# One decode step on one core: w_down's product on two partitions, one copy of it per engine, and the rounds of V in runs with the wait between them

## The chip, the cores and the metric

One NeuronCore of a Trainium2 chip. The metric is the device time of one execution in microseconds. The *span* of a trace runs from the first to the last instruction of the program that the trace records. All runs below are "fast" (none lies over 1.5% above the fastest of its kernel).

## The reference

One token goes through a pre-norm attention over a cache of 65,536 positions (8 key/value heads, 32 query heads, head size 128) and a gated block with its residual:

```python
q = (layernorm(x) @ wq)                      # x: [1, 1, 512], wq: [512, 4096]
scores = einsum("bhqd,bhkd->bhqk", q, k) * 128 ** -0.5
o = einsum("bhqk,bhkd->bhqd", softmax(scores), v)
h = x + o.reshape(1, 1, 4096) @ wo           # wo: [4096, 512]
z = layernorm(h)
out = h + (sigmoid(z @ w_gate) * (z @ w_up)) @ w_down   # F = 1792
```

K and V together are 268 MB in bf16, so this is above all a stream from memory.

## The kernel before

SyncE issues all large loads on one queue. For each head K comes in three loads and V in three (in four for the last head). VectorE transposes K by chunks, PE multiplies, ScalarE takes the exponential. The product with V runs in *rounds*: eight matmuls of 512 columns, four column groups at a time. A head has 16 rounds, ten in its first part and six in its fourth; between the sixth and the seventh, and between the fourteenth and the fifteenth, there may be a wait for the next load of V. In the code, `p` counts the rounds and is compared with `c` in every round to find the place of the wait:

```python
def waits():                       # stands away from the loop
    e.reg_alu(c, c, 8, ALU.add)
    ...                            # which wait it is; last head: "L" or "VL"
    nc.br("products", engines=here)

goto("sums", "values")             # a round begins
pv_regs(e)                         # 14 register operations: addresses
away("br_eq", p, c, "waits", waits, "products")
goto("products", "sums")
section("B")                       # eight matmuls of V
mm_at(e, ps(5, 0, 504, 96, 128), ..., kept=True)      # a spare matmul
e.reg_alu(p, p, s, ALU.add)        # ... four register operations
e.br_ne(m, 0, on_true="sums", on_false="sums_end")
```

A *spare matmul* computes nothing that is used; it is there to keep PE busy, and so its clock up. `warm(e, n)` issues n such ones of 504 columns.

The end of the kernel, after the last head (shortened):

```python
# gate and up: [1, 448] in each of four column groups, 32 matmuls
e.matmul(ps(bank, 0, FG, 32*c, 32*c + 1), lhsT=hc[:, kt:kt + 1], rhs=..., tile_position=(0, 32*c))
e.matmul(ps(YB, 0, 128), lhsT=gsel[:, :], rhs=hz[:, :], ...)      # the residual h
...                                                               # tanh, product: hh
e.transpose(hhT[:, :], hh[:, :])
# w_down: 14 row blocks r (three loads: 8, 4 and 2 blocks) x 4 column groups g
e.matmul(ps(YB, 0, 128, 32*g, 32*g + 1), lhsT=hhT[:, 32*r:32*r + 1], rhs=wd_v[:, r, g*128:(g + 1)*128], tile_position=(0, 32*g))
# g 0 and 1 copied by VectorE, 2 and 3 by ScalarE, then one row out
e.dma_start(out[0], y_sb[:, :])
```

Of the kernel before, what the change touches and what calls it, by code (L numbers as in the profile page):

```python
# [6 lines left out]
bf16 = mybir.dt.bfloat16  # L7
# [10 lines left out]
D = 512  # L18
# [197 lines left out]
def bass_sequential_preLN__gqa_block_cached__glu_gated_glu__decode_kernel(  # L216
# [21 lines left out]
    with ExitStack() as es:  # L238
# [42 lines left out]
        L_sb = sb("L_sb", [128, 4], fp32)  # L281
        lsum = sb("lsum", [128, 1], fp32)
        rl = sb("rl", [128, 1], fp32)
        hc = sb("hc", [128, 4], bf16)
        sg = sb("sg", [128, FG], fp32)
        sg2 = sb("sg2", [128, FG], fp32)
        hh = sb("hh", [128, FG], bf16)
        hhT = sb("hhT", [128, FG], bf16)
        y_sb = sb("y_sb", [1, D], bf16)

        W0 = NKT * CH
        Lw = [sb(f"Lw{i}", [128, n * DH // RW], bf16) for i, (_, n) in enumerate(WO)]
# [66 lines left out]
        op("pool", lambda e: e.iota(iota_i[:, :], [[1, 128]], base=128, channel_multiplier=-1), name="iota")  # L359
        for nm, t, v in (("onesf", onesf[:, :], 1.0), ("xz0", xz[:, :], 0.0), ("onef", one_f[:, :], 1.0), ("nhalf", nhalf[:, :], -0.5),  # L360
                         ("gs0", gsel[:, :], 0.0), ("zcol", zcol[:, :], 0.0), ("qh0", qh[:, :], 0.0), ("qz0", qz[:, :], 0.0),
                         ("PTz", PT_sb[:, 4 * 512:PT_ROW], 0.0), ("Wz", ktw[:, W0:KTW_ROW], 0.0)):
            op("pool", lambda e, t=t, v=v: e.memset(t, v), name=nm)
        op("dve", lambda e: e.tensor_scalar(ident[:, :], iota_i[:, :], 128.0, None, op0=ALU.is_equal), ["iota"], "ident")
        op("dve", lambda e: e.tensor_scalar(identf[:, :], iota_i[:, :], 128.0, None, op0=ALU.is_equal), (), "identf")
# [6 lines left out]
                                          bass.AP(tensor=head_of, offset=0, ap=[[4, 128], [0, 16], [1, 4], [0, 2]])), ["head"], "lsel")  # L372
        op("dve", lambda e: e.tensor_reduce(row_of[:, :], identf[:, :].rearrange("p (c r) -> p r c", r=RW), AX.X, ALU.max), (), "row")
        op("dve", lambda e: e.tensor_reduce(blk_of[:, :], identf[:, :].rearrange("p (c r) -> p c r", r=RW), AX.X, ALU.max), (), "blk")
        op("dve", lambda e: e.tensor_reduce(bass.AP(tensor=gsel, offset=0, ap=[[128, 128], [32, 4]]),
                                            identf[:, :].rearrange("p (s j) -> p s j", s=4), AX.X, ALU.add), ["gs0", "identf"], "gsel")



# [282 lines left out]
        def pe_flow(e, section):  # L662
            later = []

            def away(op, reg_, value, name, body, back=None):
                getattr(e, op)(reg_, value, on_true=name, on_false=f"{name}_not")
                later.append((name, body, back or f"{name}_not", blocks[-1][0]))
                label(f"{name}_not")

            i, w, p, v, m, c, s = (R.setdefault(n, e.alloc_register(f"r_{n}")) for n in "iwpvmcs")  # L670
            w0, p0 = addr_of(ktw, W0 + NC - 1 + 127), addr_of(PT_sb, 31 * 4)
            v_at = [addr_of(ring, j * CH) for j in AT["V"]]
            step = (2 * 2 * 512, 2 - 2 * 2 * 512)
            lag = v_at[0] - addr_of(ring, AT["V7"][0] * CH)
            i_last = v_at[0] - lag
            i_first = i_last + HKV * lag
            e.reg_mov(i, i_first)
            e.reg_mov(s, step[0])
            goto("head")
            e.reg_mov(w, w0)  # L680
            e.reg_mov(p, p0)
            e.reg_mov(c, p0 + 6)
            e.reg_alu(v, i, v_at[0], ALU.min)
            goto("part")
            e.br_eq(i, i_last, on_true="values", on_false="scores")
            label("scores")
            for half in range(NC // NR):
                for je in range(4):
                    if half or je:
                        e.reg_alu(reg(e, half * 4 + je), w, 2 * (je * WJ - half), ALU.add)  # L690
            away("br_eq", w, w0, "first_scores", lambda: section("As"), "more_scores")
            section("An")
            goto("more_scores", "scores")
            section("A")
            e.br_eq(i, i_first, on_true="next", on_false="values")
            label("values", "part")
            e.reg_mov(m, PARTS[0])
            warm(e, 3)
            away("br_eq", w, w0, "values0", lambda: section("V0"), "sums")
            e.br_ne(w, w0 - 12, on_true="next", on_false="values3")  # L700
            label("values3")
            e.reg_mov(v, v_at[2])
            e.reg_mov(m, PARTS[3])
            section("V3")
            goto("sums", "values")
            pv_regs(e)

            def last_second():
                section("L")

            def waits():
                e.reg_alu(c, c, 8, ALU.add)
                e.br_eq(w, w0, on_true="second", on_false="fourth")
                label("second", "waits")
                away("br_eq", i, i_last, "rows_of_o", last_second, "products")
                section("V2")
                nc.br("products", engines=here)
                label("fourth", "waits")
                e.br_ne(i, i_last, on_true="products", on_false="last_rounds")
                label("last_rounds", "fourth")  # L720
                section("VL")

            away("br_eq", p, c, "waits", waits, "products")
            goto("products", "sums")
            section("B")
            mm_at(e, ps(5, 0, 504, 96, 128), at_reg(PT_sb, reg(e, 11), [[PT_ROW, 128], [4, 32]]), e.lower_ap(qz[:, 0:504]), True, 32, 96, kept=True)
            e.reg_alu(p, p, s, ALU.add)
            e.reg_alu(s, s, step[0] ^ step[1], ALU.bitwise_xor)
            e.reg_alu(v, v, 2 * 2 * CH, ALU.add)
            e.reg_alu(m, m, -1, ALU.add)  # L730
            e.br_ne(m, 0, on_true="sums", on_false="sums_end")
            label("sums_end")
            def outs():
                warm(e, 2)
                section("O")
                warm(e, 1, load=False)

            away("br_eq", w, w0 - 12, "outs", outs)
            goto("next", "part")
            e.reg_alu(w, w, -4, ALU.add)  # L740
            e.br_ne(w, w0 - 16, on_true="part", on_false="head_end")
            label("head_end")
            e.br_eq(i, i_last, on_true="after", on_false="more_heads")
            label("more_heads")
            section("X")
            e.reg_alu(i, i, -lag, ALU.add)
            nc.br("head", engines=here)
            for name, body, back, under in later:
                label(name, under)
                body()  # L750
                nc.br(back, engines=here)
            label("after", "head_end")
# [11 lines left out]
        for i in range(HKV + 1):  # L764
            loop, last = 0 < i < HKV, i == HKV
            for r in range(NR):
# [27 lines left out]
                if not last and r == 3:  # L794
# [2 lines left out]
        P.part = {}  # L797
        regroup(1)
        project(range(NQ - GS, NQ), O3, ["O3.1", "wo1"], last=True)
        op("pe", lambda e: warm(e, 1, load=False))  # L800


        ln_stats(1, lambda e: e.tensor_tensor(hT[1][:, :], ps(YT, 0, 4), x_col[:, :], ALU.add), "yT", STB, 0)
        op("dve", lambda e: e.scalar_tensor_tensor(hc[:, :], ps(STB, 0, 1).to_broadcast([128, 4]), -1.0 / D, hT[1][:, :],
                                                   op0=ALU.mult, op1=ALU.add), ["tot.1"], "hc")
        op("dve", lambda e: e.tensor_tensor(hz[:, :].rearrange("p (j k) -> p j k", k=4),
                                            bass.AP(tensor=sel_f, offset=0, ap=[[32, 128], [1, 32], [0, 4]]),
                                            bass.AP(tensor=hT[1], offset=0, ap=[[4, 128], [0, 32], [1, 4]]), ALU.mult),
# [3 lines left out]
        for i, (nm, bank) in enumerate((("wg", GB), ("wu", UB))):  # L812
            at = W_AT[nm]
            for kt in range(4):
                for c in range(4):
                    dep = [f"{nm}.{j}" for j, (k0, _) in enumerate(W_SPLIT[nm]) if k0 == kt and c == 0]
                    op("pe", lambda e, at=at, kt=kt, c=c, bank=bank: e.matmul(  # L817
                        ps(bank, 0, FG, 32 * c, 32 * c + 1), lhsT=hc[:, kt:kt + 1],
                        rhs=ring[:, at + kt * FF + c * FG: at + kt * FF + (c + 1) * FG],
                        start=(kt == 0), stop=(kt == 3), tile_position=(0, 32 * c)),  # L820
                       ["hc"] * (kt == 0 and c == 0) + dep, f"gu{i}" if kt == 3 and c == 3 else None)
# [5 lines left out]
        op("dve", lambda e: e.tensor_tensor(hh[:, :].rearrange("p (r q) -> p r q", r=NF),  # L827
                                            ps(UB, 0, FG).rearrange("p (q r) -> p r q", r=NF),
                                            sg2[:, :].rearrange("p (q r) -> p r q", r=NF), ALU.mult), ["gu1", "sg2"], "hh")
        op("dve", lambda e: e.transpose(hhT[:, :], hh[:, :]), ["hh"], "hhT")  # L830
        for i, (r0, r1) in enumerate(WD_SPLIT):
            for r in range(r0, r1):
                for g in range(4):
                    last = r == NF - 1 and g == 3
                    op("pe", lambda e, r=r, g=g: e.matmul(  # L835
                        ps(YB, 0, 128, 32 * g, 32 * g + 1), lhsT=hhT[:, 32 * r:32 * r + 1], rhs=wd_v[:, r, g * 128:(g + 1) * 128],
                        start=False, stop=(r == NF - 1), tile_position=(0, 32 * g), skip_group_check=True),
                       ["hhT", f"wd{i}"] if r == r0 and g == 0 else (), "y" if last else None)
        for g in (0, 2, 1, 3):
            if g < 2:  # L840
                op("dve", lambda e, g=g: e.tensor_copy(y_sb[:, 128 * g:128 * g + 128], ps(YB, 0, 128, 32 * g, 32 * g + 1)), ["y"], f"ysb{g}")
            else:
                op("act", lambda e, g=g: e.activation(y_sb[:, 128 * g:128 * g + 128], ps(YB, 0, 128, 32 * g, 32 * g + 1), AF.Copy),
                   ["y"], f"ysb{g}")
        dma("sp", lambda e: e.dma_start(out[0], y_sb[:, :]), "out", [f"ysb{g}" for g in range(4)], "out")
        P.at_end = ("out",)
        P.emit()

# [27 lines left out]
```

## Time and profile before

| | |
|---|---|
| device time, median of 6 | 657.81 us (657.55 to 658.58) |
| span of the profiled run | 656.2 us |
| moved from memory | 282.33 MB, 430 GB/s over the span |
| end of the stream of loads | 653.5 us |
| mean granted PE clock | 0.872 |
| PE busy | 460.9 us (70%), of it 53.1 in the spares of the rounds |

The prediction shows the lines on which this rests: the DMA row, and the windows and the timeline of the end.

### The profile page before, as it was taken

The numbers are of one execution on the slowest core, as the hardware profiler recorded it, in microseconds if no ns is written. First come the engines' busy times: TensorE is split into PE (matmuls) and PEld (weight loads), VectorE is DVE, ScalarE is ACT, GpSimd is POOL, SyncE is SP. The second block draws the span as 40 slices with busy tenths as digits, with TensorE's granted clock in tenths as the row PEclk, the third lists the DMA queues.
The fourth block names the chain that finished last, engine by engine and source line by source line (L and its number), as shares of the span: only waits on it lengthen the run. The fifth ranks groups of instructions, "written<-read, shape, count | busy, mean of one in ns | idle before, by whom it ended". The sixth has DMA issues, their size and how long they took to land.

```text
span 656.2 us, 6578 instructions
## 1 busy us (share of the span) xinstructions
PE 460.9 (70%) x2564; PEld 73.8 (11%) x1587; DVE 350.2 (53%) x432; ACT 42.9 (7%) x114; POOL 3.6 (1%) x17
## 2 busy tenths in 40 slices
PE   0688587857669567786677676695767966777776
PEld 0200010011001010010100111010100101001122
DVE  1299846747266645647258380684536572573202
ACT  1100200020000200001000200002000020001001
POOL 1000000000000000000000000000000000000000
PEclk9989799788889697896887988787978978879798
DMA  9999999999999999999999999999999999999998
GB/s 400 431 447 431 425 421 431 431 437 433 455 431 431 431 415 434 440 443 433 421 447 431 431 423 447 446 434 437 399 447 431 431 431 431 460 434 411 425 429 348
DMA packets 8498, 282.33 MB, mean 430 GB/s; under 512 B 1073, under 2 KB 1074, under 8 KB 1586
## 3 DMA queue, kind: packets, MB, share of 16 engines
q1 hardware_dynamic: 8354, 282.33, 99.6%
q10 hardware_dynamic: 144, 0.00, 0.0%
HBM read 282.33 MB, written 0.00 MB: 430 GB/s over the span
## 4 chain that ended last, share of the span: by engine, by line
DMA 54%; PE 26%; DVE 12%; issue 6%; ACT 1%; PEldq 0%; PEld 0%; SPq 0%
DMA ring<-in_A_k_cache_dram 33%; PE PS L415 22%; DMA ring<-in_A_v_cache_dram 19%; DVE ktw L504 11%; DMA x_col<-in_A_x_dram 2%; PE PS L423 2%; ACT P_sb L550 1%; PE PS L817 0%; DVE PT_sb L560 0%; DVE M_sb L511 0%; PE PS L660 0%; PEldq L171 0%; PE PS L835 0%; PE PS L386 0%; PE PS L544 0%
## 5 line engine op out<-in xcount | busy, mean ns | idle before, releaser
L504 DVE STREAM_TRANSPOSE ktw<-ring 128x1024 f32<-128x1024 f32 x256 | 292.3, 1207 | 152.2 <-DMA ring<-in_A_k_cache_dram 152.2
L415 PE MATMUL PS<-ktw 128*128 128x512 bf16 x1024 | 287.1, 430 | 103.2 <-DVE ktw L504 86.0
L415 PE MATMUL PS<-ring,PT_sb 128*32 x1024 | 90.5, 423 | 52.6 <-PEq L171 26.8
L415 PEld LDWEIGHTS PS<-ktw 128*128 x256 | 26.7, 104 | 343.6 <-issue 246.4
L415 PE MATMUL PS<-qz,PT_sb 128*32 128x504 bf16 x128 | 53.1, 415 | 0.0
L415 PEld LDWEIGHTS PS<-ring,PT_sb 128*32 x1024 | 25.0, 115 | 134.7 <-issue 131.0
L593 ACT ACTIVATE po_sb<-PS,rl 128x512 bf16<-128x512 f32 x8 | 5.5, 687 | 524.1 <-PE PS L415 524.1
L423 PE MATMUL PS<-qz,ident 128*128 128x504 bf16 x121 | 33.7, 374 | 2.1 <-issue 2.1
L511 DVE TENSOR_REDUCE M_sb<-PS 128x1 f32<-128x512 f32 x32 | 19.9, 683 | 22.4 <-PE PS L415 22.4
L539 DVE TENSOR_REDUCE gmj<-PS 1x4 f32<-1x128 f32 x8 | 2.2, 279 | 46.0 <-PE PS L537 46.0
L550 ACT ACTIVATE P_sb<-PS,negmax 128x512 bf16<-128x512 f32 x32 | 21.6, 686 | 0.3
L560 DVE STREAM_TRANSPOSE PT_sb<-P_sb 128x512 bf16<-128x512 bf16 x32 | 20.1, 680 | 1.5 <-ACT P_sb L550 1.5
L386 PE MATMUL PS<-st,onesf 128*128 128x2 f32 x4 | 1.0, 312 | 17.1 <-DVE st L385 17.1
L415 PE MATMUL PS<-ring,xz 128*8 x32 | 9.6, 471 | 2.3 <-issue 2.3
L609 DVE TENSOR_TENSOR Lw<-O,blk_of 128x896 bf16<-128x896 bf16 (+1 forms) x2 | 1.4, 683 | 17.7 <-ACT O L599 17.7
L567 DVE TENSOR_REDUCE lsum<-PS 128x1 f32<-128x4 f32 x8 | 1.3, 162 | 17.6 <-PE PS L565 17.6
L415 PE MATMUL PS<-ktw,O 128*1 x26 | 7.5, 377 | 0.6
L423 PEld LDWEIGHTS PS<-qz,ident 128*128 128x128 bf16 x40 | 3.8, 96 | 35.3 <-issue 35.3
L544 PE MATMUL PS<-one_f,gmrep 1*128 1x1 f32 x16 | 3.2, 268 | 5.0 <-DVE gmrep L541 5.0
L468 DVE STREAM_TRANSPOSE qt<-qh 32x512 bf16<-32x512 bf16 x1 | 0.7, 700 | 11.0 <-ACT qh L465 11.0
L401 DVE CAST hT<-x_col 128x4 f32<-128x4 bf16 x1 | 0.2, 170 | 11.9 <-DMA x_col<-in_A_x_dram 11.9
L550 ACT ACTIVATION_READ_ACCUMULATOR P_sb<-PS,negmax 128x1 f32 x32 | 6.5, 203 | 0.0
(85 smaller groups left out, 73.9 us busy)
## 6 DMA issues: line engine op xcount, KB each, us to landing
ring<-in_A_k_cache_dram SPq DMA_DIRECT2D x16, 6144.0 KB, 24.4
ring<-in_A_v_cache_dram SPq DMA_DIRECT2D x15, 6144.0 KB, 24.9
ring<-in_A_v_cache_dram SPq DMA_DIRECT2D x9, 4096.0 KB, 29.6
ring<-in_A_k_cache_dram SPq DMA_DIRECT2D x8, 4096.0 KB, 24.7
ring<-in_A_wq_dram SPq DMA_DIRECT2D x1, 4096.0 KB, 12.3
ktw<-in_A_wo_dram SPq DMA_DIRECT2D x1, 3584.0 KB, 13.1
ring<-in_A_v_cache_dram SPq DMA_DIRECT2D x1, 2048.0 KB, 36.8
ring<-in_B_w_gate_dram SPq DMA_DIRECT2D x1, 1792.0 KB, 28.4
```

What stands on the lines that cost most here:

```text
L386: op("pe", lambda e: e.matmul(ps(bank, c0, c0 + 2), lhsT=onesf[:, :], rhs=st[i][:, :], start=True, stop=True), [f"st.{i}", f"sta.{i}", "on ...
L415: return e.add_instruction(mybir.InstMatmult(name=nc.get_next_instruction_name(), engine=mybir.EngineType.PE, ins=[rhs, lhsT], outs=[e.low ...
L423: e.add_instruction(mybir.InstMatmult(name=nc.get_next_instruction_name(), engine=mybir.EngineType.PE, ins=[e.lower_ap(qz[:, 0:504]), e.lo ...
L504: op("dve", lambda e, d=dst, sr=src: e.transpose(d, sr), deps, f"T{b}.{c}", to="T")
L511: op("dve", lambda e, u=u: e.tensor_reduce(M_sb[:, u % 4:u % 4 + 1], ps(u % NS, 0, 512), AX.X, ALU.max), [f"S{b}.{NC - NR + k}"], f"mx{u}" ...
L539: op("dve", lambda e: e.tensor_reduce(gmj[:, :], ps(MISC, 0, 128, 0, 1).rearrange("p (i a c) -> p a i c", a=4, c=NC), AX.XY, ALU.max), [f" ...
L544: op("pe", lambda e: e.matmul(ps(MISC, 128, 129), lhsT=gmrep[0:1, :], rhs=one_f[0:1, 0:1], start=True, stop=True), [f"gmrep{h}"], f"neg{h}")
L550: op("act", lambda e, b=b: e.activation(P_sb[:, (b % 4) * 512:(b % 4 + 1) * 512], ps(b % NS, 0, 512), AF.Exp, bias=negmax[:, k:k + 1], sca ...
L560: op("dve", lambda e, b=b: e.transpose(PT_sb[:, (b % 4) * 512:(b % 4 + 1) * 512], P_sb[:, (b % 4) * 512:(b % 4 + 1) * 512]), [f"E{b}"], f" ...
L567: op("dve", lambda e: e.tensor_reduce(lsum[:, :], ps(MISC, 132, 136), AX.X, ALU.add), [f"l{h}"], f"ls{h}", to="D")
L593: op("act", lambda e: e.activation(po_sb[:, :], ps(PO, 0, 512), AF.Copy, scale=rl[:, :]), [f"PV{h}.{NR - 1}", f"rl{h}"], f"po{h}", to="po")
L609: op("dve", lambda e: e.tensor_tensor(Lw[i][:, :].rearrange("p (j c) -> p j c", j=n), bass.AP(tensor=O2, offset=j0, ap=[[NQ, 128], [1, n], ...
```

## The change

Its intent is to shorten the end. w_down's product lands on partitions 0 and 1 of two column groups in place of one partition in each of four, so that each engine makes one copy of 128 columns and not two. To place a product on partition 1, w_down's stationary operand is two columns wide, with a column of zeros on one side; these zeros come from gate and up, whose stationary operand is padded with zeros to 32 columns. The rounds become runs of a fixed length (`m`, then `k` more), the wait is made between two runs, and the comparison in each round goes, and so does the spare. `warm` calls change from 3 to 2 in each part, and from 1 to 2 at the head's output and at the end.

```diff
-        hc = sb("hc", [128, 4], bf16)
+        hc = sb("hc", [128, 4 * 32], bf16)
-        hhT = sb("hhT", [128, FG], bf16)
-        y_sb = sb("y_sb", [1, D], bf16)
+        hhT = sb("hhT", [128, 32 + FG], bf16)
+        y_sb = sb("y_sb", [2, D // 2], bf16)
 ... hc and the first 32 columns of hhT cleared on GpSimd; gsel puts the residual on the new partitions
-            warm(e, 3)
+            warm(e, 2)
-            away("br_eq", p, c, "waits", waits, "products")
-            goto("products", "sums")
             section("B")
-            mm_at(e, ps(5, 0, 504, 96, 128), ..., kept=True)
 ...
             e.br_ne(m, 0, on_true="sums", on_false="sums_end")
             label("sums_end")
+            away("br_ne", k, 0, "waits", waits, "sums")
 ... waits(): m takes k's value, k becomes 0, and back to "sums"
             def outs():
                 warm(e, 2)
                 section("O")
-                warm(e, 1, load=False)
+                warm(e, 2, load=False)
 ...
-        op("pe", lambda e: warm(e, 1, load=False))
+        op("pe", lambda e: warm(e, 2, load=False))
 ...
-   ps(bank, 0, FG, 32 * c, 32 * c + 1), lhsT=hc[:, kt:kt + 1],
+   ps(bank, 0, FG, 32 * c, 32 * c + 32), lhsT=hc[:, 32 * kt:32 * kt + 32],
 ...
-   ps(YB, 0, 128, 32 * g, 32 * g + 1), lhsT=hhT[:, 32 * r:32 * r + 1], ..., tile_position=(0, 32 * g)
+   ps(YB, 0, 128, 32 * (g % 2), 32 * (g % 2) + 2), lhsT=hhT[:, 32 * r + 32 - g // 2:32 * r + 34 - g // 2], ..., tile_position=(0, 32 * (g % 2))
 ... four copies become two
+        op("dve", lambda e: e.tensor_copy(y_sb[:, 0:128], ps(YB, 0, 128, 0, 2)), ["y"], "ysb0")
+        op("act", lambda e: e.activation(y_sb[:, 128:256], ps(YB, 0, 128, 32, 34), AF.Copy), ["y"], "ysb1")
+        dma("sp", lambda e: e.dma_start(out[0].rearrange("o (j n) -> (o j) n", j=2), y_sb[:, :]), "out", ["ysb0", "ysb1"], "out")
```

More of the change, by code (lines that the diff above doesn't have):

```diff
@@ L361, in bass_sequential_preLN__gqa_block_cached__glu_gated_glu__decode_kernel @@
                          ("gs0", gsel[:, :], 0.0), ("zcol", zcol[:, :], 0.0), ("qh0", qh[:, :], 0.0), ("qz0", qz[:, :], 0.0),
-                         ("PTz", PT_sb[:, 4 * 512:PT_ROW], 0.0), ("Wz", ktw[:, W0:KTW_ROW], 0.0)):
+                         ("hc0", hc[:, :], 0.0), ("hhT0", hhT[:, 0:32], 0.0), ("PTz", PT_sb[:, 4 * 512:PT_ROW], 0.0), ("Wz", ktw[:, W0:KTW_ROW], 0.0)):
             op("pool", lambda e, t=t, v=v: e.memset(t, v), name=nm)
@@ L374, in bass_sequential_preLN__gqa_block_cached__glu_gated_glu__decode_kernel @@
         op("dve", lambda e: e.tensor_reduce(blk_of[:, :], identf[:, :].rearrange("p (c r) -> p c r", r=RW), AX.X, ALU.max), (), "blk")
-        op("dve", lambda e: e.tensor_reduce(bass.AP(tensor=gsel, offset=0, ap=[[128, 128], [32, 4]]),
-                                            identf[:, :].rearrange("p (s j) -> p s j", s=4), AX.X, ALU.add), ["gs0", "identf"], "gsel")
+        op("dve", lambda e: e.tensor_reduce(bass.AP(tensor=gsel, offset=0, ap=[[128, 128], [1, 2], [32, 2]]),
+                                            identf[:, :].rearrange("p (s b j) -> p s b j", s=2, b=2), AX.X, ALU.add), ["gs0", "identf"], "gsel")
         def ln_stats(i, fill, dep, bank, c0):
@@ L668, in away @@
                 label(f"{name}_not")
-            i, w, p, v, m, c, s = (R.setdefault(n, e.alloc_register(f"r_{n}")) for n in "iwpvmcs")
+            i, w, p, v, m, k, s = (R.setdefault(n, e.alloc_register(f"r_{n}")) for n in "iwpvmks")
             w0, p0 = addr_of(ktw, W0 + NC - 1 + 127), addr_of(PT_sb, 31 * 4)
@@ L681, in pe_flow @@
             e.reg_mov(p, p0)
-            e.reg_mov(c, p0 + 6)
             e.reg_alu(v, i, v_at[0], ALU.min)
@@ L696, in pe_flow @@
             label("values", "part")
-            e.reg_mov(m, PARTS[0])
-            warm(e, 3)
+            e.reg_mov(m, 6)
+            e.reg_mov(k, 4)
+            warm(e, 2)
             away("br_eq", w, w0, "values0", lambda: section("V0"), "sums")
@@ L702, in pe_flow @@
             e.reg_mov(v, v_at[2])
-            e.reg_mov(m, PARTS[3])
+            e.reg_mov(m, 4)
+            e.reg_mov(k, 2)
             section("V3")
@@ L711, in waits @@
             def waits():
-                e.reg_alu(c, c, 8, ALU.add)
+                e.reg_alu(m, k, 0, ALU.add)
+                e.reg_mov(k, 0)
                 e.br_eq(w, w0, on_true="second", on_false="fourth")
                 label("second", "waits")
-                away("br_eq", i, i_last, "rows_of_o", last_second, "products")
+                away("br_eq", i, i_last, "rows_of_o", last_second, "sums")
                 section("V2")
-                nc.br("products", engines=here)
+                nc.br("sums", engines=here)
                 label("fourth", "waits")
-                e.br_ne(i, i_last, on_true="products", on_false="last_rounds")
+                e.br_ne(i, i_last, on_true="sums", on_false="last_rounds")
                 label("last_rounds", "fourth")
                 section("VL")
-            away("br_eq", p, c, "waits", waits, "products")
-            goto("products", "sums")
             section("B")
-            mm_at(e, ps(5, 0, 504, 96, 128), at_reg(PT_sb, reg(e, 11), [[PT_ROW, 128], [4, 32]]), e.lower_ap(qz[:, 0:504]), True, 32, 96, kept=True)
             e.reg_alu(p, p, s, ALU.add)
@@ L799, in bass_sequential_preLN__gqa_block_cached__glu_gated_glu__decode_kernel @@
         project(range(NQ - GS, NQ), O3, ["O3.1", "wo1"], last=True)
-        op("pe", lambda e: warm(e, 1, load=False))
+        op("pe", lambda e: warm(e, 2, load=False))
         ln_stats(1, lambda e: e.tensor_tensor(hT[1][:, :], ps(YT, 0, 4), x_col[:, :], ALU.add), "yT", STB, 0)
-        op("dve", lambda e: e.scalar_tensor_tensor(hc[:, :], ps(STB, 0, 1).to_broadcast([128, 4]), -1.0 / D, hT[1][:, :],
-                                                   op0=ALU.mult, op1=ALU.add), ["tot.1"], "hc")
+        op("dve", lambda e: e.scalar_tensor_tensor(bass.AP(tensor=hc, offset=0, ap=[[128, 128], [32, 4]]), ps(STB, 0, 1).to_broadcast([128, 4]), -1.0 / D, hT[1][:, :],
+                                                   op0=ALU.mult, op1=ALU.add), ["tot.1", "hc0"], "hc")
         op("dve", lambda e: e.tensor_tensor(hz[:, :].rearrange("p (j k) -> p j k", k=4),
@@ L829, in bass_sequential_preLN__gqa_block_cached__glu_gated_glu__decode_kernel @@
                                             sg2[:, :].rearrange("p (q r) -> p r q", r=NF), ALU.mult), ["gu1", "sg2"], "hh")
-        op("dve", lambda e: e.transpose(hhT[:, :], hh[:, :]), ["hh"], "hhT")
+        op("dve", lambda e: e.transpose(hhT[:, 32:], hh[:, :]), ["hh", "hhT0"], "hhT")
         for i, (r0, r1) in enumerate(WD_SPLIT):
@@ L835, in bass_sequential_preLN__gqa_block_cached__glu_gated_glu__decode_kernel @@
                     op("pe", lambda e, r=r, g=g: e.matmul(
-                        ps(YB, 0, 128, 32 * g, 32 * g + 1), lhsT=hhT[:, 32 * r:32 * r + 1], rhs=wd_v[:, r, g * 128:(g + 1) * 128],
-                        start=False, stop=(r == NF - 1), tile_position=(0, 32 * g), skip_group_check=True),
+                        ps(YB, 0, 128, 32 * (g % 2), 32 * (g % 2) + 2), lhsT=hhT[:, 32 * r + 32 - g // 2:32 * r + 34 - g // 2], rhs=wd_v[:, r, g * 128:(g + 1) * 128],
+                        start=False, stop=(r == NF - 1), tile_position=(0, 32 * (g % 2)), skip_group_check=True),
                        ["hhT", f"wd{i}"] if r == r0 and g == 0 else (), "y" if last else None)
-        for g in (0, 2, 1, 3):
-            if g < 2:
-                op("dve", lambda e, g=g: e.tensor_copy(y_sb[:, 128 * g:128 * g + 128], ps(YB, 0, 128, 32 * g, 32 * g + 1)), ["y"], f"ysb{g}")
-            else:
-                op("act", lambda e, g=g: e.activation(y_sb[:, 128 * g:128 * g + 128], ps(YB, 0, 128, 32 * g, 32 * g + 1), AF.Copy),
-                   ["y"], f"ysb{g}")
-        dma("sp", lambda e: e.dma_start(out[0], y_sb[:, :]), "out", [f"ysb{g}" for g in range(4)], "out")
+        op("dve", lambda e: e.tensor_copy(y_sb[:, 0:128], ps(YB, 0, 128, 0, 2)), ["y"], "ysb0")
+        op("act", lambda e: e.activation(y_sb[:, 128:256], ps(YB, 0, 128, 32, 34), AF.Copy), ["y"], "ysb1")
+        dma("sp", lambda e: e.dma_start(out[0].rearrange("o (j n) -> (o j) n", j=2), y_sb[:, :]), "out", ["ysb0", "ysb1"], "out")
         P.at_end = ("out",)
```

## The prediction

> **What bounds the kernel now.** I read, in this order: the page's slices and queues, windows of half a microsecond over the end, the timeline of the end, windows of w_down's line alone, the landing times of the last loads, and the chain of waits from 630 us on. First the page:
>
> ```profile
> DMA  9999999999999999999999999999999999999998
> ...
> q1 hardware_dynamic: 8354, 282.33, 99.6%
> ...
> HBM read 282.33 MB, written 0.00 MB: 430 GB/s over the span
> ```
>
> One queue keeps the 16 DMA engines full in every slice but the last. A V load of 6144 KB lands in a median of 24.9 us; at 430 GB/s its 6.29 MB need 14.6 us, so it is issued with about 10 us of other transfers ahead of it. An engine that frees a buffer a few us later doesn't starve the stream, and one that frees it earlier only lengthens the queue. The first 653 us can therefore gain nothing. What can gain is what comes after the last byte. Windows (span, PE, PEld, DVE, ACT, POOL, granted clock, DMA share, GB/s):
>
> ```profile
> 649.50:650.00 0.50, 0.50 (x12) 0.26 (x8) 0.10 (x1) 0.00 (x0) 0.32 (x1) 0.50 1.00 426
> ...
> 652.50:653.00 0.50, 0.00 (x0) 0.00 (x0) 0.47 (x2) 0.00 (x0) 0.00 (x0) 0.80 0.94 369
> 653.00:653.50 0.50, 0.25 (x20) 0.25 (x24) 0.20 (x1) 0.00 (x0) 0.00 (x0) 1.00 0.75 287
> 653.50:654.00 0.50, 0.50 (x48) 0.43 (x40) 0.00 (x0) 0.00 (x0) 0.00 (x0) 1.00 0.02 8
> ```
>
> The stream ends at about 653.5, and the span at 656.2: 2.7 us are left. The timeline of them (start, length, engine, line):
>
> ```profile
> 653.25 1.01 PE L835 MATMUL PS<-ring,hhT 128*1 128x128 bf16 x56 [0.97 <-DVE hhT L830]
> 654.31 0.57 ACT L843 ACTIVATE y_sb<-PS 1x128 bf16<-1x128 f32 x2 [3.34 <-PE PS L835]
> 654.31 0.59 DVE L841 CAST y_sb<-PS 1x128 bf16<-1x128 f32 x2 [1.11 <-PE PS L835]
> 654.95 0.33 SPq L845 DMA_DIRECT2D out_dram<-y_sb  x1
> ```
>
> By this w_down's 56 matmuls wait for the transpose (L830) alone. But w_down comes in three loads, and a wait can hide inside the 56. Windows of L835 alone (span, PE, PEld, clock, DMA share, GB/s), and the landing of the last load:
>
> ```profile
> 653.85:653.90 0.05, 0.05 (x20) 0.05 (x4) 1.00 0.00 0
> 653.90:653.95 0.05, 0.05 (x16) 0.00 (x1) 1.00 0.00 0
> 653.95:654.00 0.05, 0.05 (x16) 0.03 (x8) 1.00 0.00 0
> ```
>
> ```profile
> ring<-in_B_w_down_dram SPq DMA_DIRECT2D x1, 256.0 KB, 34.8
> ```
>
> The weight loads, 8 to 12 in each window until then, stop at 653.90 and go on with a last eight at 653.95. Eight is just the two row blocks of the third load, which was issued at 619.2 and landed 34.8 us later, at about 654.0. So two things end together: the chain of compute and the last load. A faster chain can gain only until it meets that landing, which this change doesn't move.
>
> Last, the six rounds of V that close the last head, in the chain of waits:
>
> ```profile
> 637.42 0.84 PE PS L415 x9
> 638.26 0.27 issue
> 638.53 0.84 PE PS L415 x9
> 639.38 0.32 issue
> ```
>
> A round takes 1.11 to 1.17 us: eight matmuls of V, a spare one, and a gap in which PE waits for its sequencer. At 610.5 to 615.1, at half clock, the period is 1.12 to 1.19 as well, with PE never idle; so at full clock it is the sequencer's registers and branches that set the round.
>
> [...]
>
> **The change part by part.**
>
> *V's rounds in runs.* Each round loses the comparison that looked for the wait, perhaps one plain branch, and the spare matmul. [...] Before the end this is hidden[...]. In the last head it counts. V's third load landed at about 636.2 (issued near 603.8, 32 us), its rest at 641.1 (604.3 + 36.8). [...] Sum: 0.7 to 1.3 us earlier for the copy of the last head at 644.72, and for the chain behind it down to the transpose at 652.55. The two jumps away to the waits stay (1.19 us at 641.65).
>
> *Two spares more, one fewer per part.* The added ones at 645.6 and 647.4 fall in PE's idle time (up to 646.41 and 648.18) and cost nothing; they may keep the clock up for gate and up, but there the chain over VectorE and ScalarE (sg ends at 651.45) ends within 0.1 us of the matmuls, so this is worth at most 0.1.
>
> *Gate and up with 32 stationary columns.* Same columns streamed, same four groups; nothing. The two extra clears on POOL fall in the first 5 us, while x lands at 16.
>
> *w_down on two groups.* 56 matmuls over two column groups are 28 in a row instead of 14. At 53 ns: 28 x 0.053 = 1.49 plus some 0.2 of latency = 1.7 us, against 14 x 0.053 + 0.2 = 0.95 (measured 1.01). Cost 0.7 us, if the clock is full.
>
> *One copy per engine.* Two of 0.29 us become one: 0.59 - 0.29 = 0.30 saved, at the very end.
>
> *The sum.* If the chain stood as it is: + 0.7 - 0.3 = + 0.4 us. With 0.7 to 1.3 us won before it, w_down's first blocks start at about 652.3 (its first load is there at 618.2 + 33.9 = 652.1), the 24 pairs of the first two loads are done by 653.7 or so, and the last four pairs follow the landing: 654.0 + 4 x 0.053 + 0.2 = 654.4, against 654.3 now. Then 0.1 lost, 0.3 saved: - 0.2 us. I take the middle, nearer to this: - 0.1 us.
>
> **The rivals.**
> 1. *The clock.* With no spare in the rounds, PE streams 8 matmuls on four groups, 0.43 us of 1.0 (43%), where it was 0.64 of 1.15 (56%). It may then fall to half clock and do the next scores at half rate. For it: 32 score matmuls take 6.94 us at full clock, so the mean clock of 0.872 would sink. Against it: about 20 us per head in which VectorE waits for K's load (152.2 us in all), and a queue 10 us deep. Hidden unless both are used up; if it is not, 1 to 10 us more. At the end, w_down at half clock costs 28 x 0.107 = 3.0 us in place of 1.5: then + 0.8 to + 1.3 in all.
> 2. *The rounds save nothing* (a taken branch back is what costs, or the new registers cost as much). Then + 0.4 us: 658.2.
> 3. *PE frees buffers earlier and the stream gets denser.* Against it: 99.6% and a DMA share that averages near 1.0 in windows of 5 us. Worth 0.
> 4. *w_down's chain is hidden behind the last landing anyway*: - 0.2, 657.6.
>
> **Range and chances.** The outcomes with real weight are - 0.3 to + 1.3 us on a median of 657.8, whose own three runs spread from 657.55 to 658.43. So 657.7, with 656.9 to 658.8. 2% would be 13 us, five times the time after the last byte: only a starved stream could make it slower by that, and nothing could make it faster. Faster 0.01, same 0.975, slower 0.015.
>
> **What would show it right or wrong.** Right: the stream still ends at 653 to 654, DMA still 9 in all slices; rounds of about 1.0 us and the last po copy near 643.7; L835 longer (1.5 to 2 us) with its last eight right after 654; one copy of 0.29 per engine. Wrong: slices with DMA at 8 or less in the middle; rounds still at 1.15; a granted clock of 0.50 during L835; L835 no longer than 1.0, if the two groups don't serialize.

The forecast's sum: the estimate of 0.7 to 1.3 us won before the last head's copy, with rounds of about 1.0 us, + 0.7 for w_down on two groups, - 0.3 for the copies, and the last landing as the floor; it came to - 0.2 us, or + 0.4 without the rounds, and the forecast took - 0.1, so 657.7.

The times of matmuls in it can be worked out from the trace of the kernel before. 32 score matmuls of 512 columns take 6.94 us at a granted clock of 1.00 (from 124.68), so 0.217 us each; by this 128 columns take 54 ns (the text has 53), and the eight of a round, two in a row on each of four column groups, 0.43 us. At a clock of 0.50 (from 649.5) gate and up's groups of four matmuls of 448 columns, one on each column group, follow one another at 0.37 us (three in 1.12), which makes 107 ns for 128 columns. So w_down's 56 matmuls of 128 columns would take 3.0 us at full clock one after the other, and took 1.01 on four column groups. A single one of them lasts 0.22 us in the trace, 0.16 more than its 54 ns; the 0.2 of latency in the text is near to that. For gate and up the changed kernel's trace shows 0.38 us from group to group at half clock with 32 stationary columns (648.83 to 649.21), where it was 0.37 with one.

## The result

The changed kernel took 657.78 us (median of 6; 657.29 to 659.48), the kernel before 657.81. The ratio is 1.0000, with a 95% interval of 0.9987 to 1.0013. Ratios here are the mean time of one kernel's fast runs over that of the other's of the same rounds, so not quite the ratio of the medians. The predicted 657.7 was right.

From the page of the changed kernel:

```profile
PEclk9989699768788597896797887886977968877686
DMA  9999999999999999999999999999999999999997
...
q1 hardware_dynamic: 8356, 282.33, 99.5%
```

The stream is as full as before, and the clock row has more sevens and sixes: the mean granted clock fell from 0.872 to 0.823. The kernel before has this row:

```profile
PEclk9989799788889697896887988787978978879798
```

The timeline of the last head's rounds and of the end:

```profile
636.75 0.63 PE L415 MATMUL PS<-ring,PT_sb 128*32 x8 [1.43 <-PEq L171]
637.72 0.63 PE L415 MATMUL PS<-ring,PT_sb 128*32 x8 [0.34 <-issue]
638.74 2.02 PE L415 MATMUL PS<-ring,PT_sb 128*32 x16 [0.39 <-issue]
...
641.70 2.08 PE L415 MATMUL PS<-ring,PT_sb 128*32 x16 [0.94 <-DMA ring<-in_A_v_cache_dram]
...
652.32 3.15 PE L836 MATMUL PS<-ring,hhT 128*2 128x128 bf16 x56 [1.04 <-DVE hhT L831]
655.50 0.27 ACT L841 ACTIVATE y_sb<-PS 2x128 bf16<-2x128 f32 x1 [5.44 <-PE PS L836]
655.51 0.28 DVE L840 CAST y_sb<-PS 2x128 bf16<-2x128 f32 x1 [3.25 <-PE PS L836]
655.85 0.34 SPq L842 DMA_DIRECT2D out_dram<-y_sb  x1
```

Five things are to be seen. The rounds start 0.97 and 1.02 us apart, where it was 1.11 to 1.17. The fifth round, at 641.70, now waits for the last load of V and no longer for the sequencer. w_down starts 0.9 us earlier (652.32 against 653.25), as the copy of the last head's output (po) does; before and after:

```profile
644.72 0.69 ACT L593 ACTIVATE po_sb<-PS,rl 128x512 bf16<-128x512 f32 x1 [36.28 <-PE PS L415]
643.82 0.69 ACT L593 ACTIVATE po_sb<-PS,rl 128x512 bf16<-128x512 f32 x1 [35.85 <-PE PS L415]
```

w_down takes 3.15 us against 1.01. And each engine makes one copy of 0.27 or 0.28. Windows of the end (span, PE, PEld, DVE, ACT, POOL, clock, DMA share, GB/s) show why w_down is so long:

```profile
653.00:653.50 0.50, 0.50 (x16) 0.50 (x12) 0.00 (x0) 0.00 (x0) 0.00 (x0) 0.50 0.59 225
653.50:654.00 0.50, 0.50 (x16) 0.50 (x12) 0.00 (x0) 0.00 (x0) 0.00 (x0) 0.50 0.01 4
...
655.00:655.50 0.50, 0.47 (x10) 0.17 (x4) 0.00 (x0) 0.00 (x0) 0.00 (x0) 0.63 0.00 0
```

The clock is 0.50 nearly all through it; only in its last half microsecond does it come back (0.63 in the mean). The stream still ends at 653.5. So this trace shows the prediction's first rival at work, and it is the slowest of the six runs: 659.48 us, with a span of 657.1, while the six spans have a median of 656.25 and go down to 655.9. The kernel before has spans of 656.0 to 657.4, with medians of 656.25 to 656.4 in the later sets of runs. The other five runs of the changed kernel left no trace. Their shorter spans suggest that the half clock cost them less or nothing, but this is not shown. It is no rare chance: in the profiles of head6, head64, after_pad and slack below, which have the whole change and no long spares just before w_down, it ran at half clock too (w_down took 2.99 to 3.15 us).

### The profile page after: what moved, and what is told of

It is laid out like the page before. It is cut to its first block, busy times and chain, and to the rows that moved or that the text cites. A ratio compares the mean times of both kernels' runs of the same rounds, so it can differ in the third digit from the quotient of the medians.

```text
span 657.1 us, 6378 instructions
## 1 busy us (share of the span) xinstructions
PE 448.1 (68%) x2413; PEld 74.6 (11%) x1587; DVE 350.3 (53%) x431; ACT 42.6 (6%) x113; POOL 3.8 (1%) x19
## 2 busy tenths in 40 slices
DMA packets 8501, 282.33 MB, mean 430 GB/s; under 512 B 1075, under 2 KB 1077, under 8 KB 1589
## 3 DMA queue, kind: packets, MB, share of 16 engines
q1 hardware_dynamic: 8356, 282.33, 99.5%
HBM read 282.33 MB, written 0.00 MB: 430 GB/s over the span
## 4 chain that ended last, share of the span: by engine, by line
DMA 61%; PE 24%; DVE 11%; issue 3%; ACT 1%; SPq 0%; PEldq 0%; POOL 0%; DVEq 0%; ACTq 0%
DMA ring<-in_A_k_cache_dram 30%; DMA ring<-in_A_v_cache_dram 28%; PE PS L415 22%; DVE ktw L504 9%; DMA x_col<-in_A_x_dram 2%; PE PS L423 1%; PE PS L836 0%; ACT P_sb L550 0%; DVE M_sb L511 0%; PEldq L171 0%; PE PS L386 0%; DVE hh L828 0%; SPq L324 0%; SPq L342 0%; PE PS L625 0%
## 5 line engine op out<-in xcount | busy, mean ns | idle before, releaser
L415 PE MATMUL PS<-ring,PT_sb 128*32 x1024 | 94.0, 466 | 65.2 <-PEq L171 37.5
L415 PEld LDWEIGHTS PS<-ring,PT_sb 128*32 x1024 | 21.1, 117 | 132.0 <-issue 130.4
L537 PE MATMUL PS<-identf,gm 128*1 128x128 f32 x16 | 4.3, 363 | 2.2 <-DVE gm L535 2.1
```

Of the source, the lines that this page charges most:

```text
L415: return e.add_instruction(mybir.InstMatmult(name=nc.get_next_instruction_name(), engine=mybir.EngineType.PE, ins=[rhs, lhsT], outs=[e.low ...
L537: op("pe", lambda e: e.matmul(ps(MISC, 0, 128, 0, 1), lhsT=gm[:, :], rhs=identf[:, :], start=True, stop=True), [f"gm{h}"], f"gmT{h}", to="Q")
```

## The experiments

Eleven kernels ran. *Over the span* is the device time less the span, run by run, and then the median; it becomes important below. What one profiled run met by chance (above all the clock at the end) need not show in a median of spans, so both are given. Each kernel ran four times (spare_gone twice, the changed one six times).

| run | time, median | ratio to before (95%) | median span, in brackets the profiled one | over the span |
|---|---|---|---|---|
| before (three calls) | 657.74 to 657.95 | | 656.25 to 656.4 | 1.41 to 1.50 |
| changed | 657.78 | 1.0000 (0.9987, 1.0013) | 656.25 (657.1) | 1.42 |
| w_only | 658.67 | 1.0011 (0.9994, 1.0028) | 656.8 (656.8) | 1.63 |
| runs_only | 658.10 | 0.9999 (0.9982, 1.0015) | 656.5 (656.7) | 1.69 |
| four_one | 658.50 | 1.0004 (0.9987, 1.0021) | 656.4 (656.3) | 1.97 |
| after_warm | 660.50 | 1.0029 (1.0012, 1.0046) | 656.05 (656.0) | 4.52 |
| best_spare | 658.21 | 1.0006 (0.9989, 1.0022) | 656.55 (656.3) | 1.67 |
| spare_gone | 658.03 | 1.0003 (0.9983, 1.0023) | 656.65 (656.7) | 1.38 |
| slack | 669.93 | 1.0182 (1.0165, 1.0199) | 666.5 (667.6) | 4.86 |
| after_pad | 661.37 | 1.0052 (1.0036, 1.0069) | 657.0 (657.2) | 4.60 |
| head6 | 660.50 | 1.0027 (1.0002, 1.0052) | 655.9 (657.8) | 4.55 |
| head64 | 659.37 | 1.0019 (1.0001, 1.0037) | 657.75 (658.2) | 1.47 |
| warm_trim | 657.72 | 0.9998 (0.9980, 1.0016) | 656.35 (655.8) | 1.37 |

All gave the right result.

**w_only: w_down's part alone.** The kernel before, with the hunks of the diff for `hc`, `hhT`, `y_sb`, `gsel`, gate and up, w_down and the copies; rounds and spares as they were.

> Only w_down's part of the change (two column groups, padded gate and up, one copy per engine); V's rounds as before. Theory 1 (the parts cancel: faster rounds pay for a slower w_down): nothing pays here, so the transpose of the hidden vector stays near 652.6 us, w_down's 56 matmuls take 1.7 us at full clock or 3.1 at half, the copies 0.29 each, the span is 0.4 us longer (full clock) to 1.8 us longer (half), time 658.2 to 659.5. Theory 2 (the end hides behind the last load's landing, no part counts): time and span as before, 657.8.

From the timeline of w_only (start, length, engine, line and operation, number of instructions, idle time before and what ended it):

```profile
653.43 1.73 PE L835 MATMUL PS<-ring,hhT 128*2 128x128 bf16 x56 [0.96 <-DVE hhT L830]
```

The transpose ended no earlier (w_down starts at 653.43, before at 653.25), the clock was full, and two groups took 1.73 us: 0.7 more than four (1.01). The median span rose by 0.5 us, where + 0.7 for the matmuls and - 0.3 for the copies make + 0.4. So w_down's part alone is a loss by trace and span; the device times alone don't separate it from noise (the interval of the ratio holds 1).

**runs_only: the rounds and spares alone.**

```diff
 # the kernel before, with the diff's hunks in the loop over V and the warm() calls, and no others
```

> Only V's rounds in runs, with the spares as the change has them; w_down on four groups with two copies per engine as before. Theory 1: a round takes 0.96 to 1.03 us, the last head's copy (po) comes 0.9 us earlier, w_down starts at about 651.7 but its last eight matmuls still follow the last landing near 654, so the span falls by 0.2 at most: time 657.5 to 657.8. Theory 2: the same time, 657.8. A theory that the landing doesn't bind would have the span 0.9 us shorter: 656.9.

From the timeline of runs_only (PEld is the weight load of a matmul):

```profile
652.77 2.02 PE L836 MATMUL PS<-ring,hhT 128*1 128x128 bf16 x56 [1.03 <-DVE hhT L831]
653.79 0.31 PEld L836 LDWEIGHTS PS<-ring,hhT 128*1 128x1 bf16 x16 [0.29 <-DMA ring<-in_B_w_down_dram]
654.41 0.10 PEld L836 LDWEIGHTS PS<-ring,hhT 128*1 128x1 bf16 x8 [0.31 <-DMA ring<-in_B_w_down_dram]
```

w_down started earlier, and then waited for the second and the third load of its own weights: the weight loads of the last eight matmuls start as the third one lands, here at 654.41 (the stream of this run ended about half a microsecond later than others'). The clock was 0.50 all through w_down here, which also made it longer. The span didn't fall (656.5 against 656.3). A chain that is faster by itself gained nothing at this end.

**four_one: the fast rounds, four groups, and one copy of all partitions.**

```diff
-        y_sb = sb("y_sb", [1, D], bf16)
+        y_sb = sb("y_sb", [128, D // 4], bf16)
-  ... four copies, out[0] from y_sb[:, :]
+  e.tensor_copy(y_sb[:, :], ps(YB, 0, 128))               # VectorE, 128 x 128
+  e.dma_start(out[0].rearrange("o (g n) -> (o g) n", g=4), <partitions 0, 32, 64, 96 of y_sb>)
```

> As runs_only, and w_down on four groups with one copy of all 128 partitions by VectorE and an output of four rows. Theory 1: w_down's end is bound by the last landing (about 654.3), one copy of 0.28 us in place of two saves 0.3: span 0.3 to 0.4 shorter than before, time about 657.4. Theory 2: 657.8.

From the timeline of four_one, its end:

```profile
653.89 0.10 PEld L836 LDWEIGHTS PS<-ring,hhT 128*1 128x1 bf16 x8 [0.32 <-DMA ring<-in_B_w_down_dram]
654.33 0.29 DVE L840 CAST y_sb<-PS 128x128 bf16<-128x128 f32 x1 [2.12 <-PE PS L836]
654.65 0.67 SPq L841 DMA_DIRECT2D out_dram<-y_sb  x1
```

The expected 0.3 us did not come. One copy of 128 partitions costs the same 0.29 as one of a single partition, so 0.3 was saved there, and given back at once: issuing the output of four rows took 0.67 us, where one row (before) and two rows (changed) take 0.33 and 0.34.

**after_warm: three more spares just before w_down, in the changed kernel.**

```diff
         op("pe", ... matmul(ps(YB, 0, 128), lhsT=gsel[:, :], rhs=hz[:, :], ...), ["hz"])
+        for _ in range(3):
+            op("pe", lambda e: e.matmul(ps(4, 0, 504), lhsT=ident[:, :], rhs=qz[:, 0:504], start=True, stop=True, ...))
```

> The changed kernel with three more spare matmuls (504 columns) after the one that adds the residual, in the idle time of PE before w_down. If the half clock of w_down in the profiled run of the change comes from an idle stretch of 1 us before it, the clock is full in w_down: 56 matmuls in 1.7 us in place of 3.15, span about 655.8, time 657.0 to 657.4. If the clock's phase alone decides: half clock as before in w_down, about 3.1 us, and time as the changed kernel's, 657.8.

From the timeline of after_warm, w_down and its weight loads:

```profile
652.23 2.11 PE L838 MATMUL PS<-ring,hhT 128*2 128x128 bf16 x56 [0.34 <-DVE hhT L833]
653.32 0.42 PEld L838 LDWEIGHTS PS<-ring,hhT 128*2 128x2 bf16 x16 [0.22 <-DMA ring<-in_B_w_down_dram]
653.95 0.20 PEld L838 LDWEIGHTS PS<-ring,hhT 128*2 128x2 bf16 x8 [0.21 <-DMA ring<-in_B_w_down_dram]
```

For the span all came as expected: full clock, w_down waiting for its loads and done 0.4 us after the last landing, span 656.05. But the device time *rose* by 2.7 us over the changed kernel's, with 2.6 to 5.1 us over the span in place of about 1.4. No theory had this.

**spare_gone: the kernel before without the spare of each round.**

```diff
-            mm_at(e, ps(5, 0, 504, 96, 128), ..., kept=True)
```

> The kernel before without the spare matmul in each round, nothing else. Theory 1: the round falls by 0.05 us at most from 1.15, the clock falls to 0.50 in the last rounds and to a mean of about 0.82, time as before, 657.8. Rival: the round falls to 1.0 us by this alone.

From the timeline of spare_gone, four rounds of the last head:

```profile
636.95 0.63 PE L415 MATMUL PS<-ring,PT_sb 128*32 x8 [0.61 <-PEq L171]
638.09 0.63 PE L415 MATMUL PS<-ring,PT_sb 128*32 x8 [0.51 <-issue]
639.26 0.63 PE L415 MATMUL PS<-ring,PT_sb 128*32 x8 [0.53 <-issue]
640.37 0.63 PE L415 MATMUL PS<-ring,PT_sb 128*32 x8 [0.48 <-issue]
```

The rounds are still 1.11 to 1.17 us apart, with a longer gap between them: the spare cost nothing, and taking it away won nothing. The median clock fell from 0.872 to 0.816 by this alone.

**best_spare: four_one with the spare put back into the rounds.**

```diff
             section("B")
+            mm_at(e, ps(5, 0, 504, 96, 128), ..., kept=True)
```

> As four_one, with the spare matmul put back into each round. Theory 1 (branches made the round shorter, the spare held the clock): a round of about 1.00 to 1.05 us, granted clock 1.00 from 636 to 648 and a mean of about 0.87, span 0.3 us under before's: 656.0. Rival (the spare made the round longer, and the clock falls for another reason): rounds of 1.1 us or more, mean clock still 0.82.

From the timeline of best_spare, rounds of the last head with the spare (qz) in each:

```profile
637.68 0.63 PE L415 MATMUL PS<-ring,PT_sb 128*32 x8 [0.20 <-issue]
638.15 0.38 PE L415 MATMUL PS<-qz,PT_sb 128*32 128x504 bf16 x1
638.68 0.63 PE L415 MATMUL PS<-ring,PT_sb 128*32 x8 [0.15 <-issue]
...
639.73 0.63 PE L415 MATMUL PS<-ring,PT_sb 128*32 x8 [0.20 <-issue]
```

With the spare the rounds are 1.00 to 1.05 apart. With spare_gone this settles it: the comparison and the branch cost the round about 0.15 us (1.11 to 1.17 in spare_gone against 0.97 and 1.02 in the changed kernel, both without the spare), the spare some 0.03. The clock came back half of the way (median 0.851). The span, expected at 656.0, was 656.55: the end is bound by the landing and by the slow four-row output, and quicker rounds don't help there. Whether a full clock would was not seen: it fell to 0.50 at about 653.0 in this run too.

**slack: six spares in each round of the changed kernel.**

```diff
             section("B")
+            for _ in range(6):
+                mm_at(e, ps(5, 0, 504, 96, 128), ..., kept=True)
```

> The changed kernel with six spare matmuls in each round: a round of about 1.7 us at full clock (2.9 at half) in place of 1.0, so 0.75 us by 128 rounds, 96 us more of PE. Theory 1 (the stream of loads has slack, only the last two rounds count): time 1.5 to 2.5 us over the changed kernel, 659.5 to 660.5, DMA share 9 in all slices. Rival (the rounds are on the path all along): up to 96 us more, 750 us.

The DMA row of the page of slack:

```profile
DMA  9999999999999999999999999999999999999991
```

Two windows of its end (columns as above):

```profile
650.00:655.00 5.00, 5.00 (x37) 0.90 (x15) 0.00 (x0) 0.69 (x1) 0.00 (x0) 1.00 0.75 310
655.00:660.00 5.00, 4.14 (x56) 2.03 (x54) 1.87 (x12) 0.22 (x2) 0.55 (x1) 0.92 0.00 0
```

A round took 1.71 us. The stream didn't notice: it ended at 653.8 (0.75 of the five microseconds from 650), as in the other kernels. So seven heads with 16 rounds of 0.7 us more, 78 us of PE time, cost nothing. But the span grew by 10.25 us, not by 1.5 to 2.5: the expectation named the wrong rounds. All 16 rounds of the *last* head lie on the path to the end, since its first ten run before the product with wo, which runs before the last six: 16 x 0.71 = 11.4, less about 1 us in which the changed kernel waits for V's last loads. (The device time grew by 12.2 us; the rest lies over the span, as next.)

**after_pad, head6, head64, warm_trim: what lies outside the span.** after_warm added six instructions to PE's program (each matmul with its own weights counts as two). The third theory: it is the number of PE's instructions that costs the time. after_pad puts six others in the same place, head6 six and head64 sixty-four at the start of PE's program, where it waits for x anyway. warm_trim keeps two of after_warm's spares (three instructions) and takes out four elsewhere.

```diff
 # after_pad, behind the gsel matmul; head6 and head64 (63 in place of 5) ahead of project_q
+        for i in range(5):    # the first loads its weights, the others keep them
+            op("pe", <matmul of one column of qz with ident into bank 4, ldweights only for i == 0>)
 # warm_trim, behind the gsel matmul
+            <two spare matmuls of 504 columns, one load of weights>
-                warm(e, 2, load=False)                       # after the head's output
-        op("pe", lambda e: warm(e, 2, load=False))           # at the end
```

> The changed kernel with as many more PE instructions as after_warm had, in the same place, but of one column each (0.4 us in all, in PE's idle time). after_warm's measured time was 2.6 to 5.1 us over its span, where the others' was 1.3 to 2.5. If the length of PE's program sets what lies outside the span: 2.6 to 5.1 over the span here too, time 659 to 661. If it is the work of after_warm's spares: time less span 1.3 to 2.5, time about 657.8.

> The changed kernel with six more PE instructions (matmuls of one column) at the very start of PE's program, where PE waits for x some 10 us long. PE's program has 489 instructions, as after_warm's and after_pad's, against 483. Theory 3 (the length of PE's program costs time outside the span): time less span 4 to 5 us as in after_pad, time about 661. Rival (what stands near the end of the program costs it): time less span 1.4, time 657.8.

> As head6 with 64 more instructions, 547 in all. Theory 3 with a step [...]: time less span 4 to 5 us, as head6. With a slope (so much for each instruction): ten times head6's excess of 3 us, or 30 us more.

> The changed kernel with two spare matmuls before w_down, and the two behind the head's output and the two at the end taken out, so that PE's program is 482 instructions, one under the changed kernel's. Theory 3: time less span falls back to 1.4. With a full clock in w_down the span is 656.0 and the time 657.4; at half clock 657.0 and 658.4. Rival to theory 3 (spares before w_down cost it): time less span stays at 2.6 to 5.1, time 659 to 661.

In the compiled programs PE has 482 instructions before and in w_only and warm_trim, 481 in spare_gone, 483 in the changed kernel, runs_only and four_one, 484 in best_spare, 489 in after_warm, after_pad, slack and head6, and 547 in head64. The kernels with 481 to 484 lie 1.4 to 2.0 us over the span in the median, and all four with 489 lie 4.5 to 4.9 over it (single runs from 1.7 to 5.1), whether the six stand at the start of the program or at its end, and whether they do work or hardly any. warm_trim, with spares before w_down but a short program, is back at 1.37. So the theory holds between 481 and 489: six more instructions cost 3 us that the span doesn't show.

head64 went neither by the step nor by the slope. It lies only 1.47 over its span, but the span itself is 1.5 us longer, and the queues on its page have a line that the pages of the kernels of 489 instructions don't have (packets, MB, share):

```profile
q8 instruction: 1, 0.02, 0.0%
```

One packet of 0.02 MB of instructions, between 20 and 100 us. (The changed kernel and w_only have a line of that kind with 0.00 MB.) But a page ends with the span, and the trace does not. From the DMA view of head6 for 640 to 660 us:

```profile
q8 instruction: 1, 0.02, 0.3%
q14 instruction: 1, 0.01, 0.1%
```

The same view of warm_trim has the q14 packet alone. The q8 packet starts 2.1 us after the end of head6's span, and in the other three profiles of 489 instructions 2.0 to 2.3 us after it; these four runs took 4.8 to 5.0 us over the span. w_only, runs_only, spare_gone and warm_trim have no such packet after the end, and took 1.35 to 1.7. But the kernel before (659.01 us in its profiled run), the changed kernel, four_one, best_spare and head64 have one too, 1.3 to 1.9 us after the end, and took 2.0 to 2.8. So in all thirteen profiles 2.0 us or more over the span go with a late packet of instructions. The packet alone is not the 3 us, since four programs of 482 to 484 instructions have it as well.

What the late packet has to do with the length of the program is not shown. The runs show the cost and its dependence on the length (1.4 us over the span at 483 instructions in the changed kernel, 4.5 to 4.9 at 489), and the traces show the late packet; why short programs have it in some runs, why head64 with 547 instructions does not pay the 3 us, and what the rest of them is, stays open. Part of head64's longer span is the half clock that its w_down met (3.09 us).

warm_trim is the best of these, 657.72 us, with a span of 655.8 in its profile and a w_down that waits only for its loads. It doesn't beat the kernel before beyond noise (0.9998). In both profiles with long spares just before w_down (after_warm and this one) its clock was full, and in all five of the whole change without them it was half. That speaks for the spares; so few profiles don't rule out chance in the clock's timing.

## Why the prediction was right

**The number alone proves little.** The 95% interval of the ratio is about 0.9 us to each side, and holds the 658.2 and the 657.6 of the second and the fourth rival as well. That 657.78 lies so near to 657.7 is luck in part; the prediction chose its - 0.1 between - 0.2 and + 0.4 and did not work it out. What decides between the rivals are the lines of the traces.

**The stream bounds everything up to 653 us: shown.** Full slices in both kernels, the same 282.33 MB, the same end of the stream at 653.5; and slack shows that 78 us of PE time more in the first seven heads leave that end where it was.

**The rounds become 1.0 us long, and the last head's copy comes 0.7 to 1.3 us earlier: right.** 0.97 and 1.02 us; the copy at 643.82 in place of 644.72, 0.9 earlier. The sum was made of other parts than said: the four rounds before the wait ended earlier and then waited for V's last load (0.94 us idle at 641.70), so what counted was that this wait now binds, and two quicker rounds behind it. The shorter rounds refute the second rival. No trace shows a single branch; what is measured is the 0.15 us a round found by spare_gone and best_spare.

**Two groups cost 0.7 us, one copy saves 0.3: right.** 1.73 us at full clock against 1.01; 0.28 against 0.59. w_only shows + 0.5 in the span for the sum of + 0.4.

**The last landing caps the gain: shown.** In runs_only, four_one, best_spare, after_warm and warm_trim the last eight matmuls start as w_down's third load lands, between 653.8 and 654.4, whatever the chain before won. In the changed kernel's own profile it was not the landing that bound: at half clock the last matmuls came later than it.

**The first rival, the clock, came in at the end: foreseen as a rival, not in the main account.** Without the spares the mean clock fell by 0.05. In the body that was hidden. At the end w_down at half clock took 3.15 us (3.0 was given for the streaming alone), and the profiled run's span was 0.9 us over before's, inside the + 0.8 to + 1.3 that the rival was given. A clock of 0.50 during L835 (w_down; L836 in the changed kernel) was on the prediction's own list of signs of being wrong, and "1.5 to 2 us" for it and "its last eight right after 654" did not come true in that profile; after_warm and warm_trim show them, with spares added. That the time came out right all the same rests on runs without a trace, whose spans go down to 655.9. The kernel before was at half clock at 649.5 too; there PE had been busy 2.02 of the 3.4 us before it (645.9 to 649.3).

**The sum: right, and it is a sum of terms that cancel.** 0.9 us won in the chain, 0.7 lost in w_down (2.1 at half clock), 0.3 won in the copies, and a floor set by the last landing: together - 0.2 to + 0.9. What the prediction didn't see is the term of the time that lies outside the span. The change moved it by nothing (1.42 us), since it adds only one PE instruction; six more PE instructions go with 3 us, more than all its parts together.

Two later expectations were wrong, and are told above: four_one's (a four-row output gives back what one copy saves) and slack's (all rounds of the last head count, not two).

## What to carry to other kernels

Where a stream of loads is full, find its last byte first: here only work behind it could gain (78 us more of PE time ahead of it, in slack, left the stream's end at 653.8), and that work in turn can't end before the last landing plus its own consumer (w_down's last eight matmuls started at 653.8 to 654.4, as the last load landed). Look for waits inside a group of instructions, for a trace's chain names only what ended the idle time before it. And count the device time outside the span too: here six more instructions cost 3 us there, which the page of the profile doesn't show.

## What the traces add on the clock, the end of the program and small stores

- In the 3.4 us from 634.9 to 638.3 the changed kernel's PE was busy 1.63 us (48%), with no gap over 1.43 us, and the clock then fell from 1.00 to 0.50. In the kernel before PE was busy 2.44 us (72%) in the same stretch, and the clock stayed at 1.00. But the busy share alone doesn't decide: the clock fell as well after 645.1 to 648.5 in the changed kernel (PE busy 2.65 us, 78%; a clock of 0.54 in the half microsecond that follows) and after 645.9 to 649.3 in the kernel before (2.02 us, 59%; 0.50). What decides is not shown.
- With 489 PE instructions the device time less the span was 4.5 to 4.9 us in the median, with 481 to 484 it was 1.4 to 2.0 (483 in the changed kernel: 1.42).
- The issue of the output took 0.33 us for one row, 0.34 for two, 0.67 for four.
- 56 matmuls of 128 columns took 1.01 us on four column groups and 1.73 on two at full clock, 1.66 and 3.15 at half.
